# Attention and MLP block: the MLP's first input moved to SP's queue ahead of the last stores, W1 and v loads at other stages of the lead, Q loads for the maxima one slot earlier

## The chip, the core and the metric

The kernel runs on one core of a Trainium2 chip. The metric is device time in microseconds (us), the median of several runs. The engines are TensorE (PE, matmuls; PEld is its weight load), VectorE (DVE), ScalarE (ACT), GpSimd (POOL) and SyncE (SP). SP computes nothing; it issues most of the DMAs, in the order of its list, and stands still at an entry whose wait isn't met.

## The reference

```python
def _A_ref(x, wqkv, wo):                     # 1 x 2048 x 512, 32 heads of 16
    qkv = (x @ wqkv).reshape(B, S, 3, H, Dh).transpose(2, 0, 3, 1, 4)
    q, k, v = qkv[0], qkv[1], qkv[2]
    scores = einsum("bhqd,bhkd->bhqk", q, k) * (Dh ** -0.5)
    p = softmax(scores, axis=-1)
    o = einsum("bhqk,bhkd->bhqd", p, v)
    return o.transpose(0, 2, 1, 3).reshape(B, S, D) @ wo

def _B_ref(x, w1, b1, w2, b2):               # 512 -> 1792 -> 512
    h = einsum("bsd,df->bsf", x, w1) + b1
    r = where(h > 0, h, 0)
    return einsum("bsf,fd->bsd", r * r, w2) + b2

xn = layernorm(x)
out = x + _A_ref(xn, wqkv, wo) * silu(_B_ref(xn, w1, b1, w2, b2))
```

## The kernel before

Products are made from operands split in two parts, high and low, with three matmuls per product (`terms3`: high times high, high times low, low times high). Most matmuls use half of the PE's rows (64), so that two streams, called lanes, run side by side.

**Start.** Layer norm, transposes of the normed input into `xT`, and the first tiles of Q, K and V.

**Lead.** `lead_rounds` and `side_rounds` make the other Q, K and V tiles. Each tile is accumulated in PSUM, copied by ACT into `raw` (two buffers), split by POOL into `hl` (pool `hlp`, three buffers; lines L95 and L96), and stored by SP (`qk_store`, L943, into `q_d` or `k_d`) two rounds later. Between their matmuls PE makes maxima of the scores (`max_mm`, L316, reduced by DVE in L323) and, late in the lead, the first exponentials (`exp_mm`: scores L1192, then ACT L1204 into `pt`). The lead is counted in stages `g` of two maxima in each lane; 62 maxima per lane are made ahead. `mlp_early` opens buffers at stage 12; W1's first column blocks are loaded into `ex` (three buffers, `load_w1`, L453) and split by POOL into `w1s` (`split_w1`). `load_v` (L172) brings v for the first four heads. SPILLS writes `xT` out to `xn_d`. The last but one and the last tile of the lead have paths of their own: the last Q tile (`across`, in the bank `po`) is split quickly by ACT (L101) and DVE (L102) into a buffer of `hlp` and stored at once; the last K tile (`qk_done_last`) is copied by ACT into `ot` (L1012) and is split and stored some slots into the main loop.

**Main loop.** 512 slots `st`: 32 units (8 groups of four heads times four blocks of 512 queries) of 16 blocks of keys. A slot makes four maxima for later units, four exponentials, and the product of `pt` with v two slots back (L388, bank `po`). Between them lie the matmuls of the MLP (`mlp_tasks`), later those with wo. `first_pair` (L254) multiplies `xc`, a piece of 256 columns of the normed input from `xn_d`, with W1; `second` multiplies the result with W2. MLP blocks last four slots (`long_slots`). The first input `xc` is asked for at slot 2 by `load_xc(0)`, in four DMAs on ACT's queue (L503); the later ones on SP's.

**Q and K loads.** The maxima read Q from `qm` (a ring of three), the exponentials from `qe` (a ring of four). Both are loaded in pairs of heads, six DMAs each (L149), by `max_end(g)`: with `s` the stage within the unit, `qe` of unit u at s = 7 and 9, `qm` of unit u + 1 at s = 8 and 11 (unit 1 has stages of its own). A load into a ring waits until PE has read the buffer's old content.

The order of work on each engine is that of the program's text. On SP, DMAs use eight semaphores in turn, so an entry also waits for the one eight entries before it.

Of the kernel before, what the change touches and what calls it, by code (L numbers as in the profile page):

```python
# [10 lines left out]
F32R = mybir.dt.float32r  # L11
# [6 lines left out]
P = 128  # L18
# [17 lines left out]
EVAC_LAST = (1, 3, 4, 5, 7, 9)  # L36
GAPS = (18, 19, 20, 22)
FIRST = 2
SPILLS = (4, 7, 10, 13, 15, 17, 19, 21)
LAST_MAX = 486  # L40
PAIR = (484, 485)
# [12 lines left out]
def kernel(  # L54
# [11 lines left out]
    nc = tc.nc  # L66
# [44 lines left out]
    with ExitStack() as ph:  # L111
# [215 lines left out]
        def max_end(g):  # L327
            for u in [u for u, n in left.items() if n == 0]:
                del left[u]
                m4 = m4s[u % 2]  # L330
                nc.vector.tensor_reduce(m4[:, :16], mxs[u], axis=AX.X, op=ALU.max)
                mxs[u] = m4
                late.append((g + (6 if u else 0), u))
            u, s = divmod(g, 16)
            if u >= NU:
                return
            qd, qc = divmod(u, 4)
            if qc == 2 and qd + 1 < NQ and s % 2 == 0:
                load_k(qd + 1, s // 2)
            if qc == 3 and qd + 1 < NQ and s % 2 == 0 and s < 8:  # L340
                load_k(qd + 1, 8 + s // 2)
            at = (12, 14) if u == 1 else (7, 9)
            if s in at:
                load_q_pair(u, "qe", at.index(s), qes.setdefault(u, []))
            at = (6, 10) if u == 1 else (8, 11)
            if s in at and u + 1 < NU:
                load_q_pair(u + 1, "qm", at.index(s), qms.setdefault(u + 1, []))

# [119 lines left out]
        def mlp_tasks(mp):  # L468
# [29 lines left out]
            def load_xc(c):  # L498
                    xc = xp.tile([P, 2, KO, CW], F32R, name="xc")
                    for k in (0, 2) if c == 0 else (0,):  # L500
                        kos = slice(k, k + 2 if c == 0 else KO)
                        for i in range(2):
                            (nc.sync if c else nc.scalar).dma_start(  # L503
                                xc[:, i, kos].bitcast(F32), xn_d[i, :, kos, c * CW : (c + 1) * CW]
                            )
                    state["xc"] = xc
# [402 lines left out]
        pools = {}  # L909
# [89 lines left out]
        def qk_done(m, c, ps, quick, wait):  # L999
            hl = hlp.tile([P, 2, 512], F32R, name="hl")  # L1000
            if quick:
                split_psum(hl[:, 0], hl[:, 1], ps)
            else:
                raw = hlp.tile([P, 512], F32, name="raw", bufs=2)
                nc.scalar.activation(raw, ps, AF.Copy)
                split((hl[:, 0], hl[:, 1]), raw)
            later(wait, lambda: qk_store(m, c, hl))

        def qk_done_last(m, c, ps):

            raw = sp.tile([P, 512], F32, name="ot", bufs=1)
            nc.scalar.activation(raw, ps, AF.Copy)  # L1012

            def store():
                hl = pools["n"].tile([P, 2, 512], F32R, name="hl")
                split((hl[:, 0], hl[:, 1]), raw)
                later(3, lambda: qk_store(m, c, hl))

            last_store.append(store)

        def qk_first():
            tiles = [qk_tile(m, 0) for m in (4, 0)]
# [33 lines left out]
        def side_tile(spec, ps, end=None):  # L1056

            kind, a, b = spec
            if kind == "v":
                return v_terms(a, b, ps), lambda: v_done(a, b, ps, 1)  # L1060
            return qk_terms(a, b, ps), end or (lambda: qk_done(a, b, ps, False, 2))

        def side_rounds(specs, single):


            def half(tile_, lane, k):
                terms, _, first = tile_
                r = slice(64 * lane, 64 * lane + 64)
                out_, lh, rh, first_, last_ = terms[k]
                mm = nc.tensor.matmul(  # L1070
                    out_, lh(r), rh(r),
                    start=first_ and lane == first, stop=last_ and lane != first,
                    skip_group_check=True,
                )
                if k == 0 and lane != first:
                    tc.add_manual_dep(
                        mm.ins, since[first].ins.name,
                        mybir.DependencyInfo(
                            mybir.DependencyClass.Sync, mybir.DependencyReason.DATA
                        ),  # L1080
                        reason="the other row tile is done with the bank",
                    )

            n, behind, count = 3 * KO, 3 * KO // 2, len(specs) - 1
            (km, kc), tiles = specs[count][1:], {}
            ps = pv.tile([P, 512], F32, name="po")
            across = side_tile(specs[count], ps, lambda ps=ps: qk_done(km, kc, ps, True, 0)) + (1,)
            extra = [0, 0]
            for i in range(n * count + n + behind):
                if i % n == 0 and i // n < count:  # L1090
                    k = i // n
                    ps = pd.tile([P, 512], F32, name="pd_t") if k % 4 == 2 else pm.tile([P, 512], F32, name="pm_t")
                    end = None
                    if k == count - 1:
                        end = lambda ps=ps: qk_done_last(*specs[count - 1][1:], ps)
                    tiles[k] = side_tile(specs[k], ps, end) + (0,)
                for lane in range(2):
                    at = i - (n + behind) * lane
                    if 0 <= at < n * count:
                        half(tiles[at // n], lane, at % n)  # L1100
                        if lane and at % n == n - 1:
                            tiles.pop(at // n)[1]()
                        continue
                    e = extra[lane]
                    extra[lane] += 1
                    if lane:
                        if e % 3 == 2:
                            single(lane, "m")
                        else:
                            half(across, lane, e - e // 3)  # L1110
                    elif e < n:
                        half(across, lane, e)
                        if e == n - 1:
                            across[1]()
                    else:
                        single(lane, "sm"[e % 2], lambda: pm.tile([P, 512], F32, name="pm_t"))
                yield i + 1

        since = {}
        last_store = []  # L1120
# [224 lines left out]
        for g in range(LEAD):  # L1345
            shift_due(g)
            while min(made) < 2 * g + 2:
                next(rounds)
            max_end(g)
            if g == 0:  # L1350
                raw_r = [load_w("wv", 3 * P, ((D + P, 3 * P),))]
            if g == 3:
                for ko in range(KO):
                    split_w(wr_t, ko, slice(3 * P, 6 * P), raw_r[0][:, ko])
                ln.close()
                pools["v"] = ph.enter_context(tc.tile_pool(name="vp", bufs=1))
            if g == 12:
                s1.close()
                ep = ph.enter_context(tc.tile_pool(name="ep", bufs=1))
                rot["pt"] = [ep.tile([P, 512], F32, name=f"pt{i}") for i in range(NPT)]  # L1360
                pools["n"] = ph.enter_context(tc.tile_pool(name="np", bufs=1))
                mlp_early()
            if g in (18, 20):
                split_w1((g - 18) // 2)
                load_w1(3 + (g - 18) // 2)
            if g == 16:
                for fo in range(3):
                    load_w1(fo)
                load_v(0)
        for _ in rounds:  # L1370
            pass
# [161 lines left out]
        for st_ in range(NU * 16):  # L1533
            if st_ < done:
                continue
            begin(st_)
            if st_ == FIRST:
                qs.close()
            item = next(dn, None)
            if st_ == FIRST:  # L1540

                for g in (LEAD, LEAD + 1):
                    max_end(g)
                later(4, last_store.pop())
            if item is not None and len(item) > 2:
                assert st_ % 4 == 0
                long_slots(st_, *item[:2])
                done = st_ + 4
                continue
            if item is not None and item[0] is not None:  # L1550
                slot(st_, *item)
            else:

                plain_slot(st_)
                flip[0] += 1
            shift_due(st_ + 1 + LEAD)
            pv_step(st_ - 2, pts.pop(st_ - 2))
# [32 lines left out]
```

## Time and profile before

| | |
|---|---|
| median of 3 runs | 1638.53 us (1638.46 to 1638.76) |
| profiled execution, its own time | 1639.71 us |
| profiled execution, span | 1637.9 us |
| granted PE clock, mean over the span | 0.998 |
| HBM read, written | 149.95 MB, 56.61 MB |

In the profile's rows a start is counted from the span's first instruction. "SPq" and "ACTq" are DMA issues by SP and ACT, whose duration is that of the issue, not of the transfer. A row of a timeline gives start, duration, engine, line, operation, output and inputs, count, and in brackets the idle time before it with what ended it. A row of a stretch gives for each engine its busy time, with the count of its instructions, then the granted PE clock as a share of the full one, the busy share of the DMA engines, and GB/s. Two lanes run at once, so PE counts as busy when one of them stands.

### The profile page before, as it was taken

To read this page: it belongs to the slowest core of one execution; us is meant where nothing else is said; L and a number is where in the kernel's file an instruction comes from. 1 tells how busy PE (TensorE), PEld (TensorE's weight loads), DVE (VectorE), ACT (ScalarE), POOL (GpSimd) and SP (SyncE) were. 2 spreads that over 40 slices of the span, in tenths; PEclk is the share of its full clock that TensorE was granted. 3 is DMA by queue.
4 is the path that set the end of the run, shared out by engine and by line. 5 is a ranking of instruction groups with operands and counts; after the bars stand their busy time and mean duration, and the time that the engine had idled before them with its cause. 6 is when DMAs were issued, how large, how long until landed. Compare 5 with 4: busy or idle time off the path is not lost.

```text
span 1637.9 us, 36064 instructions
## 1 busy us (share of the span) xinstructions
PE 1617.7 (99%) x13684; PEld 941.6 (57%) x13684; DVE 1358.0 (83%) x2346; ACT 1189.5 (73%) x2351; POOL 523.3 (32%) x547
## 2 busy tenths in 40 slices
PE   8999999999999999999999999999999999999998
PEld 6898565456545654665566446644664565545543
DVE  6486788888888888888888988888888888887744
ACT  7212577777777777777777777777777777777786
POOL 6437568123212211231132113311331133225421
PEclk9999999999999999999999999999999999999999
DMA  6787555424333433433433334423442252246654
GB/s 229 222 277 256 176 184 154 117 85 143 81 86 98 125 75 97 122 96 82 105 108 98 87 93 118 120 63 89 136 114 52 85 156 76 56 129 198 200 171 155
DMA packets 163941, 209.22 MB, mean 128 GB/s; under 512 B 59448, under 2 KB 78392, under 8 KB 162232
## 3 DMA queue, kind: packets, MB, share of 16 engines
q1 hardware_dynamic: 162392, 205.35, 43.4%
q8 instruction: 108, 1.77, 0.5%
q10 hardware_dynamic: 1376, 1.57, 0.3%
q14 instruction: 65, 0.53, 0.1%
HBM read 149.95 MB, written 56.61 MB: 126 GB/s over the span
## 4 chain that ended last, share of the span: by engine, by line
PE 93%; ACT 3%; DMA 2%; SPq 1%; DVE 1%; POOL 1%; issue 0%; ACTq 0%; POOLq 0%; DVEq 0%
PE po L388 30%; PE pd_t L254 19%; PE pm_t L316 17%; PE se L1192 14%; PE pd_t L222 5%; PE pm_t L1070 3%; ACT pt L1204 2%; PE se L1040 1%; PE se L988 1%; DMA xc<-xn_d 1%; PE pd_t L1070 1%; DMA k_d<-hl 1%; PE se L316 1%; SPq L149 0%; PE pm_t L1154 0%; PE pd_t L1040 0%
## 5 line engine op out<-in xcount | busy, mean ns | idle before, releaser
L323 DVE TENSOR_REDUCE mx<-pm_t 128x1 f32<-128x512 f32 x1927 | 1196.9, 683 | 173.5 <-PE pm_t L316 83.9
L1204 ACT ACTIVATE pt<-se 128x512 f32<-128x512 f32 x1996 | 1043.2, 617 | 261.2 <-PE se L1192 214.0
L316 PE MATMUL pm_t<-ka,qm 64*128 64x512 f32 x1927 | 770.7, 420 | 2.5 <-DMA qm<-q_d 1.8
L1192 PE MATMUL se<-qe,ka 64*128 64x512 f32 x1996 | 672.9, 396 | 2.0 <-ACT pt L1204 2.0
L388 PE MATMUL po<-pt,v 128*32 128x512 f32 x4096 | 545.5, 605 | 0.0
L316 PEld LDWEIGHTS pm_t<-ka,qm 64*128 64x128 f32 x1927 | 338.6, 184 | 240.7 <-DVE mx L323 224.8
L254 PEld LDWEIGHTS pd_t<-xc,w1s 64*128 64x128 f32 x2688 | 335.4, 187 | 96.4 <-issue 89.0
L254 PE MATMUL pd_t<-xc,w1s 64*128 64x256 f32 x2688 | 382.1, 289 | 1.9 <-DMA xc<-xn_d 1.9
L1192 PEld LDWEIGHTS se<-qe,ka 64*128 64x128 f32 x1996 | 337.2, 185 | 22.0 <-ACT pt L1204 4.7
L254 PE MATMUL pd_t<-w2t,hT 64*128 64x512 f32 x1080 | 300.7, 411 | 0.0
L254 PEld LDWEIGHTS pd_t<-w2t,hT 64*128 64x128 f32 x1080 | 179.1, 184 | 83.0 <-issue 75.5
L546 POOL TENSOR_TENSOR r<-r 128x512 f32<-128x512 f32 x56 | 58.2, 1040 | 378.9 <-ACT r L543 378.9
L388 PEld LDWEIGHTS po<-pt,v 128*32 128x32 f32 x4096 | 81.0, 108 | 158.9 <-issue 136.5
L565 POOL TENSOR_TENSOR u<-u,b_t 128x512 f32<-128x512 f32 x16 | 20.6, 1286 | 318.4 <-ACT u L564 284.6
L426 POOL TENSOR_TENSOR ot<-ot,hl 128x512 f32<-128x512 f32 x31 | 39.9, 1287 | 201.9 <-DMA hl<-r_d 132.9
L323 DVE TENSOR_REDUCE mx<-se 128x1 f32<-128x512 f32 x121 | 77.9, 686 | 28.3 <-PE pm_t L1070 15.2
L222 PE MATMUL pd_t<-wot,oc 64*128 64x512 f32 x336 | 91.1, 407 | 0.0
L543 ACT ACTIVATE r<-pd_t,b_t 128x256 f32<-128x256 f32 x112 | 46.9, 470 | 57.1 <-PE pd_t L254 55.9
L222 PEld LDWEIGHTS pd_t<-wot,oc 64*128 64x128 f32 x336 | 58.2, 184 | 45.9 <-ACT pt L1204 12.6
L1070 PE MATMUL pm_t<-xT,wr_t 64*128 64x512 f32 x408 | 74.2, 388 | 0.0
L96 POOL TENSOR_TENSOR hT<-r,hT 128x512 fp32r<-128x512 f32 x56 | 72.3, 1291 | 4.7
L222 PE MATMUL pd_t<-w2t,hT 64*128 64x512 f32 x264 | 68.9, 393 | 0.0
(131 smaller groups left out, 1069.4 us busy)
## 6 DMA issues: line engine op xcount, KB each, us to landing
w1s<-w_d SPq DMA_DIRECT2D x196, 256.0 KB
qm<-q_d SPq DMA_DIRECT2D x384, 32.0 KB
ka<-k_d SPq DMA_DIRECT2D x96, 128.0 KB
qe<-q_d SPq DMA_DIRECT2D x384, 32.0 KB
k_d<-hl SPq DMA_DIRECT2D x16, 512.0 KB
q_d<-hl SPq DMA_DIRECT2D x16, 512.0 KB
xn_d<-xT SPq DMA_DIRECT2D x8, 1024.0 KB
g<-g_d SPq DMA_DIRECT2D x32, 256.0 KB
```

Source lines behind the costliest of these rows:

```text
L96: (lo or nc.gpsimd).tensor_tensor(dst[1], raw, dst[0].bitcast(F32), op=ALU.subtract)
L222: mm = nc.tensor.matmul(out_, lh(r), rh(r), start=first_ and lane == 0, stop=last_ and lane == 1, skip_group_check=True,)
L254: mm = nc.tensor.matmul(out_, lh(r), rh(r), start=first_ and lane == 0, stop=last_ and lane == 1, skip_group_check=True,)
L316: nc.tensor.matmul(ps, qms[u][p][64 * j : 64 * j + 64, qb * P : (qb + 1) * P], kas[qd, p][64 * j : 64 * j + 64, kc * 512 : (kc + 1) * 512] ...
L323: return nc.vector.tensor_reduce(mxs[u][:, c, kc : kc + 1], ps, axis=AX.X, op=ALU.max)
L388: nc.tensor.matmul(po[32 * j : 32 * j + 32, :], vs[qd][:, (4 * kb + j) * VW : (4 * kb + j) * VW + 32], pts[j], start=(kb == 0), stop=(kb = ...
L426: nc.gpsimd.tensor_tensor(ot, ot, hl[:, 1].bitcast(F32), op=ALU.mult)
L543: nc.scalar.activation(r[:, i], ps[:, i * CW : (i + 1) * CW], AF.Relu, bias=b1_t[:, fo : fo + 1])
L546: nc.gpsimd.tensor_tensor(r, r, r, op=ALU.mult)
L1070: mm = nc.tensor.matmul(out_, lh(r), rh(r), start=first_ and lane == first, stop=last_ and lane != first, skip_group_check=True,)
L1192: nc.tensor.matmul(se, kas[qd, j // 2][b : b + 64, kb * P : (kb + 1) * P], qes[u][j // 2][b : b + 64, :], start=True, stop=True,)
L1204: return nc.scalar.activation(pts[j], se, AF.Exp, scale=0.25)
```

## The change

- `load_xc(0)` issues its four DMAs on SP's queue, like the later ones. They stand there behind the lead's stores and ahead of the store of the last Q tile and of the Q loads that slot 2 asks for.
- The last Q tile (`qk_done_across`) is split into a buffer of the pool `n` in place of `hlp`, and its store is asked for at slot 2, behind `xc`. The last K tile's split and store use the same single buffer after it.
- W1's five first loads go out at stages 13, 14, 16, 20 and 23 in place of three at 16, one at 18 and one at 20; v at 18 in place of 16; the second W1 split at 21 in place of 20.
- `qm`'s first pair is asked for at s = 7 and `qe`'s first pair at s = 8, in place of 8 and 7.

The order of PE's and DVE's instructions is as before, and so is ACT's but for the four DMA issues. On SP the lead's stores and loads come in the text's order; before, some Q loads of the first slots stood among the lead's last stores, and now these stand behind `xc`.

```diff
+W1_LOADS = (13, 14, 16, 20, 23)
...
-            at = (12, 14) if u == 1 else (7, 9)
+            at = (12, 14) if u == 1 else (8, 9)
             if s in at:
                 load_q_pair(u, "qe", at.index(s), qes.setdefault(u, []))
-            at = (6, 10) if u == 1 else (8, 11)
+            at = (6, 10) if u == 1 else (7, 11)
             if s in at and u + 1 < NU:
                 load_q_pair(u + 1, "qm", at.index(s), qms.setdefault(u + 1, []))
...
                         for i in range(2):
-                            (nc.sync if c else nc.scalar).dma_start(
+                            nc.sync.dma_start(
                                 xc[:, i, kos].bitcast(F32), xn_d[i, :, kos, c * CW : (c + 1) * CW]
                             )
...
-            last_store.append(store)
+            last_store.append(lambda: later(4, store))
+
+        def qk_done_across(m, c, ps):
+            hl = pools["n"].tile([P, 2, 512], F32R, name="hl")
+            split_psum(hl[:, 0], hl[:, 1], ps)
+            last_store.append(lambda: qk_store(m, c, hl))
...
-            across = side_tile(specs[count], ps, lambda ps=ps: qk_done(km, kc, ps, True, 0)) + (1,)
+            across = side_tile(specs[count], ps, lambda ps=ps: qk_done_across(km, kc, ps)) + (1,)
...
-            if g in (18, 20):
-                split_w1((g - 18) // 2)
-                load_w1(3 + (g - 18) // 2)
-            if g == 16:
-                for fo in range(3):
-                    load_w1(fo)
+            if g in W1_LOADS:
+                load_w1(W1_LOADS.index(g))
+            if g in (18, 21):
+                split_w1((g - 18) // 3)
+            if g == 18:
                 load_v(0)
...
-                later(4, last_store.pop())
+                for fn in last_store:
+                    fn()
```

## The prediction

> **What bounds the kernel now.** I read the busy table first, then the waits of TensorE (PE), then the stretches of the span, then the timelines around each stretch in which PE is not full.
>
> ```profile
> span 1637.9 us, 36064 instructions
> PE 1617.7 (99%) x13684; PEld 941.6 (57%) x13684; DVE 1358.0 (83%) x2346; ACT 1189.5 (73%) x2351; POOL 523.3 (32%) x547
> ```
>
> PE is idle for 1637.9 - 1617.7 = 20.2 us in all. A change that leaves PE's instructions alone can win only there, and in time when PE runs below its pace. This one leaves them alone: PE, DVE and the activations keep their instructions and their order, only DMAs, some GpSimd (POOL) work and one evacuation's buffer move. So the question is which of these stretches it touches.
>
> ```profile
> core 0: us, PE busy (x) PEld busy (x) DVE busy (x) ACT busy (x) POOL busy (x), PEclk, DMA share, GB/s
> 138.00:150.00 12.00, 10.92 (x90) 8.94 (x88) 6.07 (x10) 3.78 (x8) 11.18 (x14) 1.00 0.88 307
> 170.00:181.00 11.00, 7.34 (x51) 3.36 (x49) 6.58 (x11) 5.71 (x11) 7.67 (x12) 0.98 0.97 297
> 177.00:180.40 3.40, 1.67 (x15) 0.96 (x11) 1.39 (x2) 1.28 (x3) 1.19 (x1) 1.00 1.13 340
> 180.40:183.80 3.40, 3.19 (x23) 2.97 (x27) 2.04 (x3) 1.42 (x3) 0.00 (x0) 0.53 0.48 125
> 184.00:319.00 135.00, 135.00 (x1190) 77.28 (x1186) 117.75 (x199) 102.70 (x205) 78.57 (x98) 1.00 0.49 146
> 318.90:322.30 3.40, 1.61 (x15) 0.72 (x15) 1.60 (x5) 1.44 (x3) 0.00 (x0) 1.00 0.35 101
> 322.00:1570.00 1248.00, 1248.00 (x10802) 689.02 (x10800) 1094.84 (x1864) 962.40 (x1907) 330.28 (x320) 1.00 0.39 107
> ```
>
> Between 184 and 1570 us PE is full but for one hole at 320. The three places to win are the end of the lead (138 to 150), the passage from the lead to the main loop (170 to 184, where the granted clock also falls to 0.53 for 3.4 us), and the hole at 320. The rest of the idle time lies at the first load and in the tail, which the change does not touch.
>
> **A: W1 and v loads spread over the lead.**
>
> ```profile
> 126.32 2.13 SPq L453 DMA_DIRECT2D ex<-in_B_w_dram  x3
> 128.50 0.59 SPq L172 DMA_DIRECT2D v<-v_d  x1
> ```
>
> ```profile
> 129.19 8.71 DMA k_d<-hl
> 167.13 2.78 DMA k_d<-hl
> ```
>
> ```profile
> 131.18 0.60 ACT L1005 ACTIVATE raw<-pd_t 128x512 f32<-128x512 f32 x1 [2.61 <-PE pd_t L1070]
> 140.07 0.60 ACT L1005 ACTIVATE raw<-pm_t 128x512 f32<-128x512 f32 x1 [4.25 <-POOL hl L96]
> ...
> 149.47 0.60 ACT L1005 ACTIVATE raw<-pm_t 128x512 f32<-128x512 f32 x1 [2.04 <-PE se L316]
> 152.69 0.60 ACT L1005 ACTIVATE raw<-pm_t 128x512 f32<-128x512 f32 x1 [2.13 <-PE se L316]
> ```
>
> The first fence is SP's queue, the second the chain of work (start, duration, what), the third ScalarE's timeline. Three W1 loads and the v load go out at once; the K store right behind them takes 8.71 us instead of 2.78. POOL's split waits for that store's buffer (three in the ring), the copies `raw` (two) wait for POOL, and the exponentials queued behind `raw` on ScalarE keep PE's banks. Both outer rows end a wait for PE, so they show PE's pace: a tile takes 152.69 - 149.47 = 3.22 us, and the five between 131.18 and 149.47 (135.22, 140.07, 144.41 and 146.34 lie in between) took 18.29, not 16.10. The loss is 2.2 us, of which 12 - 10.92 = 1.08 shows as idle; in the rest one of PE's two row halves ran alone. After the change W1 goes out at stages 13, 14, 16, 20 and 23 and v at 18, with at least one store between any two; the second W1 split on POOL comes one tile later. The v load's own delay stays, just before the exponentials begin: of the extra 8.71 - 2.78 = 5.9 us its 544 KB of 1312 KB (three loads of 256 KB and v) make 2.5 us, an estimate by bytes.
>
> ```profile
> 169.48 0.62 POOL L95 TENSOR_SCALAR hl<-raw 128x512 fp32r<-128x512 f32 x1 [0.41 <-ACT raw L1005]
> 170.18 1.30 POOL L96 TENSOR_TENSOR hl<-raw,hl 128x512 fp32r<-128x512 f32 x1
> ```
>
> POOL works 0.62 + 1.30 us in a tile of 3.22 and so makes up 1.3 us per tile, and the second copy gives another tile: most of 2.5 us is taken up before PE feels it. I take 0.3 us as left: gain **1.9**, bounds 2.2 and, if v hits the exponentials squarely (a rival below), 0; below zero would need more bytes at once than the 1312 KB of before, which the spreading excludes.
>
> **B: the passage, up to the MLP's first matmul.**
>
> ```profile
> 170.01 0.60 ACT L101 ACTIVATE hl<-po 128x512 fp32r<-128x512 f32 x1 [0.62 <-DMA k_d<-hl]
> ...
> 172.01 3.08 ACTq L503 DMA_DIRECT2D xc<-xn_d  x3
> 175.13 2.07 ACT L1204 ACTIVATE pt<-se 128x512 f32<-128x512 f32 x4 [2.57 <-PE pm_t L316]
> ```
>
> ```profile
> 172.04 0.49 PE L316 MATMUL pm_t<-ka,qm 64*128 64x512 f32 x1 [0.64 <-DVE mx L323]
> ...
> 175.78 0.50 PE L1192 MATMUL se<-qe,ka 64*128 64x512 f32 x1 [0.99 <-ACT pt L1204]
> ...
> 177.21 0.38 PE L254 MATMUL pd_t<-xc,w1s 64*128 64x256 f32 x1
> 178.37 0.38 PE L254 MATMUL pd_t<-xc,w1s 64*128 64x256 f32 x1 [0.67 <-DMA xc<-xn_d]
> ...
> 180.61 0.58 PE L254 MATMUL pd_t<-xc,w1s 64*128 64x256 f32 x1 [1.27 <-DMA xc<-xn_d]
> ...
> 183.68 1.20 PE L388 MATMUL po<-pt,v 128*32 128x512 f32 x8
> ...
> 186.94 0.50 PE L316 MATMUL pm_t<-ka,qm 64*128 64x512 f32 x1
> ...
> 189.53 1.06 PE L388 MATMUL po<-pt,v 128*32 128x512 f32 x8
> ```
>
> ScalarE issues the four transfers of `xc` itself: from 172.01 it stands at the last three for 3.08 us, and its exponentials go on at 175.13, which costs PE 0.99. On SP these issues are off ScalarE. The 0.64 is DVE being late: its half of the last tile's split follows ScalarE's at 170.01, which had waited for a K store's buffer. The tile now writes another buffer, so the wait goes; but only 0.62 us of ScalarE idleness lies there and part of it is PE finishing the tile, so I take 0.4. B: 0.99 + 0.4 = **1.4** of 1.63, bounds 0.9 and 1.63.
>
> **C: the wait for `xc`, and the clock.** From the first MLP matmul to the first `po` group: 183.68 - 177.21 = 6.47 us; the same part of the block at full pace takes 189.53 - 186.94 = 2.59. Loss 3.9 us: 0.67 + 1.27 of waits, about 3.19/2 = 1.6 of half clock, 0.4 of lone row halves. When does `xc` land from SP's queue?
>
> ```profile
> 171.87 0.86 SPq L943 DMA_DIRECT2D k_d<-hl  x1
> ```
>
> ```profile
> k_d<-hl SPq DMA_DIRECT2D x16, 512.0 KB
> ...
> xc<-xn_d ACTq DMA_DIRECT2D x4, 256.0 KB
> ```
>
> SP takes its list in order, and the last entry before `xc` is the K store (issued at 171.87 here) that waits for POOL's split, done at 170.18 + 1.30 = 171.5. That store lands after some 2.8 us, at 174.3; the four pieces behind it need 0.262 MB / 340 GB/s (the row from 177.00) = 0.77 us each, so they land at about 175.1, 175.8, 176.6 and 177.4. Before, the last landed by 180.6, because the same engines also moved another Q store of 512 KB, two W1 loads and six of Q: these now stand behind `xc` on SP. PE comes to the first matmul at 177.21 - 1.4 = 175.8, needs the second piece at once and the other two after six terms, which took from 178.37 to 180.61 - 1.27 = 179.34, about 1 us. So the fourth piece is late by 0.6 us; that much waiting remains. The half clock: it came behind a stretch with PE busy 1.67 of 3.40. The stretch 318.90 to 322.30 has 1.61 of 3.40 and no lower clock after it, so the trigger is not the share alone; with 0.6 us of waits instead of 1.9, and B's also gone, I take the fall as gone. C: 3.9 - 0.6 = **3.3**, bounds 0 and 3.9.
>
> What is queued behind SP's new wait (for PE's last matmul that reads the memory `xc` takes): the Q store of the last tiles, `qm` and `qe` loads of the next units and two W1 loads. The nearest need is `qm`: 62 maxima per row half are made ahead, two more in each slot from 2 on, and its pair begins with number 80, nine slots on, at 5.8 us for two slots (189.53 - 183.68) some 26 us later. The last K tile now shares one buffer with the tile before and its split waits for that store; POOL has no other work there until the first MLP activation, and nothing near reads that K.
>
> **D: Q for the maxima one slot sooner.**
>
> ```profile
> 297.42 1.73 SPq L435 DMA_DIRECT2D on_d<-hl  x4
> 307.12 2.63 SPq L149 DMA_DIRECT2D qe<-q_d  x6
> 309.79 1.46 SPq L172 DMA_DIRECT2D v<-v_d  x1
> ...
> 314.14 3.96 SPq L149 DMA_DIRECT2D qm<-q_d  x6
> ```
>
> ```profile
> 321.75 0.46 PE L316 MATMUL pm_t<-ka,qm 64*128 64x512 f32 x1 [1.79 <-DMA qm<-q_d]
> ```
>
> SP was free from 299.2 but stood until 307.12 at the `qe` load, whose buffer PE was still reading. `qm` came behind that, behind v and two `xc` pieces. Swapped, `qm` finds its buffer long free (its last maxima lie some 12 slots back) and goes out near 299.2; even if it takes the 7.6 us that it took here (314.14 to 321.75) it is there at 307, 13 us before PE asks (321.75 - 1.79 = 319.96). `qe` goes one slot later, and its unit starts 16 slots after. The swap is made in nearly all 32 units; elsewhere PE shows no such hole, so it neither gains nor costs there. D: **1.8**, bounds 1.5 and 1.8.
>
> **Sum.** 1.9 + 1.4 + 3.3 + 1.8 = 8.4 us. After 184 us PE is the full engine (135.00 of 135.00), so each us won ahead arrives at the end. The profiled execution took 1639.71 us, its span 1637.9: span after 1629.5, that execution 1631.3. The median shown is 1638.53, 1.2 below the profiled one: **1630.1**.
>
> **The rivals.**
> 1. `xc` still comes late and the clock falls as before: C brings nothing, 1638.5 - (1.9 + 1.4 + 1.8) = 1633.4. It decides if SP reaches `xc` 3 us later than I take it, for example one POOL tile of 3.22 us behind. Against: POOL ended the last split 0.1 us after PE's last tile. [...] Chance 0.14.
> 2. The clock falls although the waits go: 1.6 less, 1631.7. What speaks for it: the longest single wait before the fall was only 1.27 us, and a hole of 1.79 at 320 made no fall, so the waits need not be its cause. [...] Chance 0.08.
> 3. The lead's stall moves: v now lands among the first exponentials, A brings nothing: 1632.0. Chance 0.09.
> 4. Slower: SP's one list. If POOL falls two tiles (6.4 us) behind in the lead, SP stands at its stores, and two more of them than in my sum (1.05 MB, 3.1 us) go out at once ahead of `xc`, whose last piece lands at 177.4 + 6.4 + 3.1 = 186.9, against a need at 177: 9.9 us of waiting and a window at half clock (1.7) in place of C's 3.9. With B won, D won and A's loss kept: 1638.5 + 11.6 - 3.9 - 1.4 - 1.8 = 1643.0. The balance tips at a wait of 7.1 - 1.7 = 5.4 us (7.1 is C, B and D together), a lag of some 3.4 us with its share of stores, and it is slower by over 0.2% from about 5.6 us; POOL would have to lose that where the spreading should save. Chance 0.05.
> 5. The gain is swallowed (a new wait in the 31 reordered units, 0.27 us in each): 1638.5. Against: every other unit has PE full in either order. Chance 0.06.
>
> **How the numbers follow.** Forecast 0.58, rivals 0.14, 0.08, 0.09, 0.05, 0.06. A measurement of this kernel can tell about 0.2% (3.3 us) from no change, so faster means under 1635.2: forecast and rivals 1 to 3 nearly whole, 0.88 with a little taken off for a mix of 1 and 3; same 0.07; slower 0.05. All losses gone would be 2.2 + 1.63 + 3.9 + 1.8 = 9.5, or 1629.0; the low end is 1628.8. The high end takes in rivals 1 and 3 together, 1635.3.
>
> **What would show it.** Right: PE's holes at 141 and 145, 172 to 181 and 320 gone or under 0.7 us, no stretch with clock under 1.00 between 60 and 1620, no K store over 6 us, `qm` issued before v near 300. Wrong: `xc` landing after 179, ScalarE's `raw` waiting for POOL beyond 150, a new PE wait for `qe` or `qm`.

## The result and the profile after

| | before | changed |
|---|---|---|
| median (runs) | 1638.49 us (8) | 1633.93 us (8) |
| lowest to highest | 1637.21 to 1641.77 | 1633.35 to 1635.61 |
| profiled execution, its own time | 1639.71 us | 1634.46 us |
| profiled execution, span | 1637.9 us | 1632.7 us |

The ratio is 0.9971, interval 0.9961 to 0.9982. The change made the kernel faster by 4.6 us. The forecast was 1630.1 us, a gain of 8.4; the direction and the range held, the size was about twice too large.

The busy table of the changed kernel has the same work on every engine. PE's idle time is 1632.7 - 1616.6 = 16.1 us, where it was 20.2.

```profile
span 1632.7 us, 36089 instructions
PE 1616.6 (99%) x13684; PEld 943.5 (58%) x13684; DVE 1358.6 (83%) x2346; ACT 1189.7 (73%) x2351; POOL 523.3 (32%) x547
```

The waits of PE (total us, times, longest):

```profile
PE pd_t L255 <- DMA xc<-xn_d: 1.5, 3, 0.7
...
PE pd_t L223 <- DMA oc<-on_d: 0.4, 1, 0.4
PE pm_t L317 <- DVE mx L324: 0.4, 1, 0.4
PE se L1198 <- ACT pt L1210: 0.3, 1, 0.3
```

The wait for `qm` (1.8) is gone, that for ScalarE's exponentials has fallen from 2.0 to 0.3, and a wait for `oc` is new. The wait for `xc` should have fallen to 0.6 and stands at 1.5. The same stretches as in the prediction, for the changed kernel:

```profile
core 0: us, PE busy (x) PEld busy (x) DVE busy (x) ACT busy (x) POOL busy (x), PEclk, DMA share, GB/s
138.00:150.00 12.00, 12.00 (x108) 11.93 (x106) 7.37 (x12) 4.07 (x8) 10.24 (x13) 1.00 0.78 245
170.00:181.00 11.00, 9.40 (x62) 4.44 (x60) 6.97 (x12) 5.47 (x10) 5.81 (x9) 0.84 0.69 221
177.00:180.40 3.40, 3.40 (x27) 2.25 (x25) 1.99 (x3) 1.79 (x3) 1.89 (x2) 0.57 0.29 82
180.40:183.80 3.40, 3.40 (x30) 1.58 (x28) 2.00 (x4) 1.58 (x3) 0.00 (x0) 0.93 0.58 154
184.00:319.00 135.00, 135.00 (x1190) 77.42 (x1186) 119.50 (x203) 104.47 (x208) 78.56 (x98) 1.00 0.57 162
318.90:322.30 3.40, 3.40 (x30) 1.41 (x24) 2.71 (x6) 2.03 (x4) 0.00 (x0) 1.00 0.02 5
322.00:1570.00 1248.00, 1247.27 (x10792) 687.61 (x10790) 1092.17 (x1859) 962.51 (x1909) 332.76 (x321) 1.00 0.39 106
```

PE is full at 138 to 150 and at 320, where the holes were. The half clock is still there: at 177.00 to 180.40 the granted clock is 0.57 and in the next stretch 0.93, so (0.43 + 0.07) x 3.4 = 1.7 us of PE time are lost.

To place the gain I cut the way to the steady loop at four events of PE's timeline: the first matmul of the side tiles, the end of the lead's last matmul, the first MLP matmul (T0), and the second `po` group after T0. "Half clock" says whether the stretch behind T0 has a window of some 3.4 us with the granted clock near 0.5. The runs with names are told in the next section.

| profile | start | lead | end of lead to T0 | T0 to second `po` group | half clock |
|---|---|---|---|---|---|
| before | 62.78 | 108.62 | 5.81 | 8.73 | yes |
| e10, before again | 64.65 | 106.94 | 6.02 | 8.55 | yes |
| changed | 62.89 | 106.42 | 4.28 | 8.57 | yes |
| e7, changed again | 63.20 | 106.32 | 4.24 | 6.87 | no |
| e11, changed, third | 63.60 | 106.32 | 4.42 | 6.77 | no |
| e1, Q swap alone | 64.23 | 106.88 | 5.87 | 7.33 | no |
| e2, loads spread alone | 63.81 | 106.30 | 5.76 | 8.51 | yes |
| e3, passage alone | 64.29 | 107.88 | 4.15 | 8.73 | yes |
| e6, `xc` on SP alone | 64.39 | 106.71 | 5.50 | 8.59 | yes |
| e4, K store behind `xc` | 63.19 | 106.40 | 4.12 | 6.49 | no |
| e12, both stores behind | 63.27 | 106.40 | 4.13 | 5.76 | no |
| e8, order of terms | 64.60 | 106.31 | 4.12 | 5.82 | no |
| e9, swap to unit 27 | 64.19 | 106.32 | 4.11 | 4.70 | no |
| e5, a quarter of `xc` | 64.40 | 106.31 | 4.35 | 4.71 | no |

The first pair of profiles differs by 5.2 us: 2.2 in the lead (A), 1.5 up to T0 (B), 0.2 behind T0 (C), 1.8 at 320 (D), less 0.1 for a later start and 0.45 for the wait for `oc` near 1513. Step C, forecast at 3.3, brought nothing in this execution.

### The profile page after: what moved, and what is told of

Its sections match the earlier page's. It is cut to its first block, busy times and chain, and to the rows that moved or that the text cites. A ratio compares the mean times of both kernels' runs of the same rounds, so it can differ in the third digit from the quotient of the medians.

```text
span 1632.7 us, 36089 instructions
## 1 busy us (share of the span) xinstructions
PE 1616.6 (99%) x13684; PEld 943.5 (58%) x13684; DVE 1358.6 (83%) x2346; ACT 1189.7 (73%) x2351; POOL 523.3 (32%) x547
## 4 chain that ended last, share of the span: by engine, by line
PE 98%; DVE 1%; DMA 1%; SPq 0%; issue 0%; ACT 0%; POOL 0%; DVEq 0%; POOLq 0%; ACTq 0%
PE po L389 31%; PE pd_t L255 19%; PE pm_t L317 17%; PE se L1198 14%; PE pd_t L223 6%; PE pm_t L1076 4%; PE pd_t L1076 1%; PE se L1046 1%; PE se L989 1%; PE se L317 1%; PE pm_t L1198 1%; PE pm_t L1160 0%; DVE mx L324 0%; PE pd_t L1046 0%; PE pm_t L829 0%; DMA xc<-xn_d 0%
```

## The experiments

Ratios are to the kernel before, timed on the same chip.

| kernel | median us (runs) | ratio, interval | span of its profile |
|---|---|---|---|
| e1, Q swap alone | 1637.02 (10) | 0.9991, 0.9982 to 1.0000 | 1635.7 |
| e2, loads spread alone | 1638.04 (10) | 0.9996, 0.9987 to 1.0005 | 1636.1 |
| e3, passage alone | 1635.45 (10) | 0.9982, 0.9973 to 0.9991 | 1635.7 |
| e6, `xc` on SP alone | 1638.05 (11) | 0.9999, 0.9990 to 1.0008 | 1636.3 |
| e7, changed again | 1633.01 (7) | 0.9972, 0.9961 to 0.9983 | 1630.6 |
| e4, K store behind `xc` | 1631.79 (5) | 0.9964, 0.9951 to 0.9976 | 1629.9 |
| e12, both stores behind | 1631.58 (5) | 0.9963, 0.9948 to 0.9977 | 1629.3 |
| e8, order of terms | 1632.24 (5) | 0.9963, 0.9950 to 0.9975 | 1631.6 |
| e9, swap to unit 27 | 1632.36 (8) | 0.9969, 0.9959 to 0.9980 | 1629.8 |
| e5, a quarter of `xc` | 1630.18 (5) | 0.9952, 0.9939 to 0.9966 | 1629.1 |

**e1 to e3: the three parts, one at a time.** Each is the kernel before with one part of the change.

```diff
 e1:
-            at = (12, 14) if u == 1 else (7, 9)      # qe
+            at = (12, 14) if u == 1 else (8, 9)
...
-            at = (6, 10) if u == 1 else (8, 11)      # qm
+            at = (6, 10) if u == 1 else (7, 11)
 e2:
+W1_LOADS = (13, 14, 16, 20, 23)
...
-            if g in (18, 20):
-                split_w1((g - 18) // 2)
-                load_w1(3 + (g - 18) // 2)
-            if g == 16:
-                for fo in range(3):
-                    load_w1(fo)
+            if g in W1_LOADS:
+                load_w1(W1_LOADS.index(g))
+            if g in (18, 21):
+                split_w1((g - 18) // 3)
+            if g == 18:
                 load_v(0)
 e3:
-                            (nc.sync if c else nc.scalar).dma_start(
+                            nc.sync.dma_start(
...
+        def qk_done_across(m, c, ps):
+            hl = pools["n"].tile([P, 2, 512], F32R, name="hl")
...
```

> The kernel before with the Q swap alone (qm's first pair at s = 7, qe's at s = 8). Theory: the hole of 1.79 us at 320 goes and nothing else moves, span 1637.9 - 1.8 = 1636.1, the passage at 170 to 184 and its half clock as before. Rival (the swap only moves the wait, to qe or to another load): a new PE wait of over 1 us somewhere after 300, span near 1637.9.

> The kernel before with W1 and v loads spread alone. Theory: the lead's last matmul ends near 169.3 in place of 171.4, PE without idle between 126 and 165, then the passage and the hole at 320 as before, span 1637.9 - 2.1 = 1635.8. Rival (the passage takes it back: xc meets the same stores and comes no sooner): lead's end 2.1 us sooner, but the first po group of the MLP's first block still at 183.7, span near 1637.9.

> The kernel before with xc on SP and the last Q tile's other buffer and later store, without the other parts. Theory (xc stands behind a K store of 512 KB on SP and still lands late, the clock falls): first MLP matmul 1.5 us sooner after the lead's end than before (4.3 us in place of 5.8), some 1.5 us of waits for xc, a half-clock window, span 1637.9 - 1.7 = 1636.2. Rival (the passage's gain in the changed kernel came only because the lead ran smoothly): no gain, 1637.9.

The swap brings 1638.63 - 1637.02 = 1.6 us (interval 0 to 2.9), the loads 0.6 with an interval that takes in none, the passage 3.2 (1.5 to 4.4). Together 5.4, about what the whole change gives (0.9971 and 0.9972 are 4.6 to 4.8); within this noise there is no sign that the parts fight each other. In the profiles each part does its own work: with the swap the hole at 320 is gone, with the spread the lead is 106.30, and with the passage the second stage is 4.15.

**e6: `xc` on SP, and nothing else.** The last Q tile keeps its buffer and is stored at once, so its store stands ahead of `xc`.

```diff
-                            (nc.sync if c else nc.scalar).dma_start(
+                            nc.sync.dma_start(
```

> The kernel before with xc on SP alone, the last Q tile stored at once as before and so ahead of xc with the K store. Theory (what counts is the bytes ahead of xc on SP): ScalarE is free, so the first MLP matmul comes 4.5 us after the lead's end in place of 5.8; xc stands behind 1 MB and waits come to about 3 us (1.6 us more than in the changed kernel), so nearly all of the 1.3 us is given back; span 1637.9 within 1. Rival (freeing ScalarE is all that the move brings, the order behind the stores does not matter): waits as in the changed kernel, 1.5 us, span near 1636.2.

It brings nothing that can be measured. SP's queue, and PE's timeline behind it:

```profile
167.97 3.35 SPq L943 DMA_DIRECT2D q_d<-hl  x2
171.42 0.42 SPq L943 DMA_DIRECT2D k_d<-hl  x1
171.93 3.31 SPq L503 DMA_DIRECT2D xc<-xn_d  x4
```

```profile
176.60 0.35 PE L254 MATMUL pd_t<-xc,w1s 64*128 64x256 f32 x1 [0.82 <-POOL hl L95]
177.17 0.39 PE L254 MATMUL pd_t<-xc,w1s 64*128 64x256 f32 x1 [0.22 <-DMA xc<-xn_d]
```

ScalarE is freed here too, but `xc` now stands in SP's list behind a K store that waits for POOL's last split, and the last Q tile's 512 KB go out ahead of it too. The row puts the 0.82 down to POOL, whose split just before it, from 175.94 to 176.56, is that of the last K tile; these matmuls read only `xc` and `w1s`, so I take it for the wait for the first piece of `xc`. What ScalarE no longer loses is lost at T0 instead: the stage to T0 takes 5.50, only 0.3 to 0.5 below the profiles of before. The other buffer and the later store of the last Q tile, taken together, are what make the move pay (4.15 in e3); no run has one without the other.

**e4, e5 and e12: what stands beside `xc`.** The changed kernel with edits at the passage only. e4 holds the K store that goes out just ahead of `xc` (its tile in a buffer of v that is not yet used) and stores it behind `xc`. e12 also asks for that store and for the last Q store two slots later. e5 loads only the first of the four parts of the first `xc` and uses it for all four; it shows the passage without a wait for `xc`.

```diff
 e4:
+        def qk_done_held(m, c, ps):
+            raw = hlp.tile([P, 512], F32, name="raw", bufs=2)
+            nc.scalar.activation(raw, ps, AF.Copy)
+            hl = vs["tiles"][1][:, :1024].bitcast(F32R).rearrange("p (a n) -> p a n", a=2)
+            split((hl[:, 0], hl[:, 1]), raw)
+            last_store.append(lambda: qk_store(m, c, hl))
...
+                    if k == count - 2:
+                        end = lambda ps=ps: qk_done_held(*specs[count - 2][1:], ps)
 e12, on e4, in qk_done_held and in qk_done_across:
-            last_store.append(lambda: qk_store(m, c, hl))
+            last_store.append(lambda: later(2, lambda: qk_store(m, c, hl)))
 e5:
-                    for k in (0, 2) if c == 0 else (0,):
-                        kos = slice(k, k + 2 if c == 0 else KO)
+                    for k in (0,):
+                        kos = slice(k, k + 1 if c == 0 else KO)
...
-                            lambda b, q, ko=ko: xc[q, b, ko],
+                            lambda b, q, ko=ko: xc[q, b, ko if c else 0],
```

> The changed kernel, with the last K store that stands ahead of xc on SP moved behind it: that tile is split into the second v tile, free until slot 48, and stored after xc. Theory (the 512 KB ahead cost xc 1.6 us, and the waits bring the half clock): waits for xc under 0.4 us in place of 1.5, no half-clock window before 1620, span 1632.7 - 1.2 - 1.7 = 1629.8. Rival 1 (the waits aren't the cause of the half clock): waits gone but the window at 0.5 stays, span 1631.4. Rival 2 (xc is late by its own start and pace, not by the store): waits stay at 1.5 us, span 1632.7.

> The changed kernel, but the first input of the MLP is loaded for a quarter only (two pieces of 128 KB), and the first piece's matmuls all read that quarter: it leaves out three quarters of the first load, so the wait for xc is taken away by less data. Theory (the half clock comes from PE's waits around xc): PE waits for xc under 0.3 us in all, from the first MLP matmul to the second po group some 4.9 us, no half-clock window before 1620, span 1632.7 - 3.6 = 1629.1. Rival (the clock falls for the thin work of slots 2 and 3, whatever xc does): the window at 0.5 stays in most executions, mean clock 0.999 or less, span near 1630.8.

> As e4_store_behind, but the held K store and the last Q tile's store are asked for two slots later, so that they stand behind the six qm loads (0.2 MB) in SP's list: nothing but these small loads is then in flight while xc (four pieces, 1.05 MB) moves. In e4 the pieces were still 0.78 + 0.30 = 1.1 us late. Between 170.5 and 176.4 us its DMA engines moved 5.90 us x 315 GB/s = 1.86 MB, 0.8 MB more than xc has, so the stores behind xc in SP's list were served before xc's last piece. Theory (the stores behind take their share of the engines): without them xc and qm are 1.25 MB, 3.7 us at 340 GB/s from the start of transfers, so the last piece lands some 2 us sooner than in e4 and PE's waits for xc are under 0.3 us; the stage from the first MLP matmul to the second po group after it takes 4.7 to 5.4 us instead of 6.5. Rival (xc's own pace: it is slow whatever stands behind it, by its short rows or its issues): the waits stay at 0.8 to 1.1 us, the stage at 6.2 to 6.6, and GB/s in that stretch falls to about 200. By the median 1630.0 to 1631.5 by the theory, 1631.5 to 1632.5 by the rival, with the spread between executions making the stage the better sign.

First the changed kernel itself: SP's queue, PE's timeline, and the stretches of the passage with the bytes that the DMA engines moved (last column).

```profile
169.41 0.36 SPq L944 DMA_DIRECT2D k_d<-hl  x1
169.88 2.47 SPq L504 DMA_DIRECT2D xc<-xn_d  x4
172.45 0.41 SPq L944 DMA_DIRECT2D q_d<-hl  x1
172.91 3.68 SPq L150 DMA_DIRECT2D qm<-q_d  x6
```

```profile
169.74 0.50 PE L317 MATMUL pm_t<-ka,qm 64*128 64x512 f32 x1 [0.44 <-DVE mx L324]
...
173.59 0.35 PE L255 MATMUL pd_t<-xc,w1s 64*128 64x256 f32 x1
174.51 0.38 PE L255 MATMUL pd_t<-xc,w1s 64*128 64x256 f32 x1 [0.57 <-DMA xc<-xn_d]
...
176.19 0.35 PE L255 MATMUL pd_t<-xc,w1s 64*128 64x256 f32 x1 [0.72 <-DMA xc<-xn_d]
176.76 0.38 PE L255 MATMUL pd_t<-xc,w1s 64*128 64x256 f32 x1 [0.21 <-DMA xc<-xn_d]
...
182.16 1.06 PE L389 MATMUL po<-pt,v 128*32 128x512 f32 x8
```

```profile
169.50:170.00 0.50, 0.26 (x2) 0.19 (x2) 0.50 (x2) 0.50 (x2) 0.42 (x2) 1.00 0.00 0
170.00:171.50 1.50, 1.40 (x12) 0.34 (x10) 1.50 (x4) 1.50 (x3) 1.42 (x3) 1.00 0.83 298
171.50:174.50 3.00, 2.44 (x18) 0.77 (x14) 2.63 (x5) 1.10 (x3) 2.50 (x5) 1.00 0.92 262
174.50:176.80 2.30, 1.35 (x11) 0.87 (x11) 0.84 (x2) 1.08 (x2) 0.00 (x0) 1.00 0.99 355
```

The list is in the order that was meant. But by 176.8 us, when the last piece of `xc` is there, the engines have moved 1.50 x 298 + 3.00 x 262 + 2.30 x 355 = 2050 KB, where the K store and `xc` are 524 + 1049 = 1573 KB. The other 0.48 MB, 1.4 us at 340 GB/s (the kernel before, 177.00 to 180.40), can only be what was issued behind `xc`: the Q store at 172.45 and the `qm` loads. So the engines were working on later entries before PE had the last piece. But 0.48 MB is only the most that can have been served ahead of `xc`. Had everything gone in the order of the list, the 1573 KB would have been through by about 175.5 (1.50 x 298 + 3.00 x 262 + 1.0 x 355), and the other 1.3 us would then be time between the last byte and PE's start. The trace does not say which bytes were whose, so the two accounts are not told apart here.

e4 and e12, PE's timeline in each:

```profile
175.68 0.35 PE L255 MATMUL pd_t<-xc,w1s 64*128 64x256 f32 x1 [0.78 <-DMA xc<-xn_d]
176.34 0.38 PE L255 MATMUL pd_t<-xc,w1s 64*128 64x256 f32 x1 [0.30 <-DMA xc<-xn_d]
```

```profile
175.71 0.38 PE L255 MATMUL pd_t<-xc,w1s 64*128 64x256 f32 x1 [0.48 <-DMA xc<-xn_d]
```

In e4 the waits are 1.1 us, against 1.2 to 1.5 in the three profiles of the changed kernel, and the stage behind T0 is 6.49, against 6.8 to 6.9 in the two without half clock. In e12 they are 0.48 and 5.76. Without any wait for `xc` the stage is 4.71 (e5), so late data costs 2.1 us in the changed kernel (6.77 and 6.87 less 4.71). The medians bear that out: e5 lies 2.8 us below e7, taken on the same chip (1630.18 against 1633.01), and every execution of e5 is faster than every one of e7. How those 2.1 us divide between the store ahead, the stores beside and `xc` itself is not shown. Each step is a difference of two single profiles, and e8 and e9 below, which have the same passage, differ by more (5.82 and 4.70). PE's timeline in e8, then in e9:

```profile
177.71 0.38 PE L255 MATMUL pd_t<-xc,w1s 64*128 64x256 f32 x1 [0.35 <-DMA xc<-xn_d]
```

```profile
176.15 0.40 PE L255 MATMUL pd_t<-xc,w1s 64*128 64x256 f32 x2
```

These rows are the fourteenth term of e8 and the thirteenth and fourteenth of e9, the first to read the last two pieces. SP issues `xc` from 170.94 on in e8 and from 170.53 on in e9. So from the first issue of `xc` to its last piece pass 6.77 us in e8, as in e4 (6.72), but under 5.9 in e9, whose list on SP is the same, with both stores right behind `xc`. That is no longer than in e12 without them (6.00). And e4 and e12 have the same ratio by the median (0.9964 and 0.9963). So e12 does not decide between the two theories that I gave it. The stretches of e12 show how the load runs when nothing but the `qm` loads stands beside it:

```profile
170.00:171.00 1.00, 0.79 (x4) 0.37 (x4) 1.00 (x3) 1.00 (x3) 0.92 (x3) 1.00 0.20 48
171.00:172.00 1.00, 1.00 (x10) 0.16 (x8) 1.00 (x3) 0.87 (x2) 0.92 (x2) 1.00 1.00 331
...
174.00:175.00 1.00, 1.00 (x11) 0.72 (x9) 0.88 (x3) 0.44 (x1) 0.57 (x1) 1.00 0.57 188
175.00:176.00 1.00, 0.52 (x4) 0.32 (x6) 0.61 (x2) 0.64 (x2) 0.00 (x0) 1.00 0.44 158
```

`xc` was asked for from 169.71 on; little moves before 171, the engines are full for 3 us, and then they stand half empty while PE waits until 175.71. The forecast had 1.26 us for start and end together, inside the 2.8 us that it gave the K store (2.8 less 524 KB at 340 GB/s); what makes the slow start and end was not tried.

**e8: the order of the terms.** On e4, the first MLP pair multiplies what has already landed before what is still missing.

```diff
+                if c == f == 0:
+                    mms = mms[:6] + mms[12:18] + mms[6:12] + mms[18:]
```

> The changed kernel with the last K store behind xc, and in the first MLP pair both column halves use the first two pieces of xc before either uses the last two: twelve terms in place of six are done before the third piece is needed, one more us of work. Theory: the waits that the store behind xc left (0.78 and 0.30 us) go, from the first MLP matmul to the second po group about 5.2 us in place of 6.49, span 1629.9 - 1.1 = 1628.8. Rival (the waits were partly hidden by the other row half, so the order changes nothing): span 1629.9.

The stage behind T0 falls from 6.49 to 5.82, but, as said, it is 4.70 in e9 with the same passage, so one profile does not give the size of the step. By the median nothing is gained over e4 (ratios 0.9963 and 0.9964). The profile of e8 shows a loss at another place. PE's timeline, SP's queue, and the chain of waits:

```profile
1512.39 0.49 PE L223 MATMUL pd_t<-wot,oc 64*128 64x512 f32 x1 [0.82 <-DMA oc<-on_d]
```

```profile
1503.96 4.02 SPq L150 DMA_DIRECT2D qe<-q_d  x6
1508.02 0.42 SPq L676 DMA_DIRECT2D oc<-on_d  x1
```

```profile
1505.23 0.42 SPq L150
1505.69 1.82 SPq L150
1507.55 0.42 SPq L150
```

The later `qe` load of the swap stands ahead of an `oc` load in SP's list, and one of its six issues takes 1.82 us instead of 0.42. The wait for `oc` is 0.45 in the first profile of the changed kernel, 0.60 in e1, and absent in e4, e5, e7, e11 and e12. None of the profiles without the swap has it, so it goes with the swap, in some executions. Slow issues alone do not make it: in e4 the same six take 3.88 us together, against 4.02 in e8 and 2.61 in e11, and PE has no wait.

**e9: the swap only up to unit 27,** on e8, to free that place.

```diff
-            at = (12, 14) if u == 1 else (8, 9)
+            at = (12, 14) if u == 1 else (8, 9) if u < 28 else (7, 9)
...
-            at = (6, 10) if u == 1 else (7, 11)
+            at = (6, 10) if u == 1 else (7, 11) if u < 28 else (8, 11)
```

> The kernel with the store behind xc and the new order of terms, and the Q swap only up to unit 27; the last units load qe first again, as before. Theory (the late wait for oc, 0.4 to 0.8 us near 1510 in three profiles with the swap, comes from the two qe loads now standing together ahead of that oc piece): no wait for oc over 0.2 us, the oc piece asked for some 1.5 us sooner against PE, span 0.5 to 0.8 less than with the swap throughout. Rival (that wait depends on other traffic): it stays.

The wait for `oc` is gone, and one for `qm` stands late in the loop instead. From the waits of PE in e9:

```profile
PE pm_t L317 <- DMA qm<-q_d: 0.3, 1, 0.3
```

No gain follows. Of the versions that leave nothing out, e4 and e12 have the lowest medians, but their intervals and that of the changed kernel overlap.

**e7, e10 and e11: the same kernels again,** to see what differs between executions of one program.

> The changed kernel once more, for a second profile. [...] Rival (the fall is fixed in the program's order): the same window behind xc as in the first profile.

> The kernel before once more, for a second profile. Theory (the lead's loss and the fall of the clock differ from execution to execution): the lead takes between 106.5 and 108.6 us from its first side matmul to its last, waits for xc again near 2 us, the hole at 320 again 1.0 to 1.8 us; the half clock as it falls. Rival (both are fixed): 108.6 and a half-clock window again.

> The changed kernel a third time, for its profile. Theory: the lead takes 106.3 to 106.5 us again, waits for xc 1.3 to 1.5 us, and the half clock as it falls, with a span near 1632.7 where it does and near 1631 where it doesn't. Rival: the lead's time or the waits for xc vary as much as in the kernel before.

e7 waits for `xc` nearly as long as the first profile of the changed kernel (1.3 against 1.5), in the same places. Its stretch behind the waits:

```profile
176.00:179.40 3.40, 2.98 (x28) 1.95 (x28) 1.89 (x3) 1.57 (x3) 1.14 (x2) 1.00 0.59 211
```

The clock is 1.00. So the fall is not fixed by the program. In e11 the clock is 1.00 as well, with 1.2 us of waits. The stage behind T0 is 6.87 without the fall and 8.57 with it: 1.7 us, the same as worked out from the granted clock. Among the profiles with 1.2 us or more of waits for `xc`, six have the window (before, e10, e2, e3, e6, changed; granted clock 0.91 from 165 to 184) and three have not (e1 with 2.0 us of waits, e7, e11; 1.00 there); of the five with 1.1 us or less (e4, e5, e8, e9, e12; 1.00 there) none has.

e10 shows that the kernel before differs too: its lead takes 106.94, not 108.62. Its span is 1638.3 us, that of e11 1630.8; both were run once.

## Why the prediction was right or wrong

**Direction, and the rule that a us won ahead arrives at the end: right.** PE is full from 184 to 319 and nearly so to 1570, and the stage gains of the first pair of profiles add up to the difference of the spans within 0.1 us.

**A, 1.9: the mechanism right, the size the top of what occurs.** ScalarE's timeline of the changed kernel:

```profile
131.29 0.60 ACT L1006 ACTIVATE raw<-pd_t 128x512 f32<-128x512 f32 x1 [2.56 <-POOL w1s L97]
...
147.38 0.60 ACT L1006 ACTIVATE raw<-pm_t 128x512 f32<-128x512 f32 x1 [2.15 <-PE pm_t L1076]
150.59 0.60 ACT L1006 ACTIVATE raw<-pm_t 128x512 f32<-128x512 f32 x1 [2.12 <-PE pm_t L1076]
```

Five tiles take 147.38 - 131.29 = 16.09 us, the pace of 3.22 each, and from 147 on the copies wait for PE. All of the 2.2 came; the 0.3 that I kept back for v did not show. But the nine profiles with the spread have a lead of 106.30 to 106.42, and the five with the old loads 106.71 to 108.62, mean 107.4: the stall that I measured was the largest of the five. On average A is worth 1.1, and e2's median agrees (0.6, with an interval from -0.8 to 2.1 us). The step that failed is "the loss is 2.2 us", read from one execution and taken for all.

**B, 1.4: the sum right, one term too large.** It measured 1.5 to 1.6. ScalarE's stop of 0.99 at T0 is gone. DVE's 0.64, counted with 0.4 for the new buffer, is only down to 0.44, and e6, which keeps the old buffer, has 0.49; the other 0.3 of B lies elsewhere in the passage and was not placed. e6 adds that without the last Q tile's new buffer and later store hardly any of B is left.

**C, 3.3: mis-sized.** In the first profile it brought 0.2. Two steps failed. The first is "so they land at about 175.1, 175.8, 176.6 and 177.4", that is, the last 5.9 us after POOL's split, which lets the K store go. The K store went out as early before T0 as forecast (173.59 - 169.41 = 4.2, forecast 175.8 - 171.5 = 4.3), so rival 1's condition, SP reaching `xc` 3 us late, did not hold. The last piece came 176.76 - 169.41 = 7.4 us after that store, and 7.2 in e7 and e11: 1.3 to 1.5 later than forecast. I gave `xc` the full 340 GB/s in the order of the list; the engines moved less (262 GB/s from 171.5 to 174.5), and up to 0.48 MB of what they moved was not ahead in the list. How much of the delay is this share, and how much is time between the last byte and PE's start, stays open. The waits were 1.2 to 1.5 in place of 0.6.

The second is "I take the fall as gone". It came in one of three profiles of the changed kernel, and in e3, which has the same passage. Rival 2 had it come although the waits go; the waits had not gone, so it was not put to the test. Where they did fall below 1.2 us (e4, e5, e8, e9, e12), no profile has the fall. The four profiles with the old passage (before, e10, e1, e2) take 8.3 us on average behind T0, the four with the new one (changed, e7, e11, e3) 7.7, so C is 0.5 by these; the fall came in three of the first four and two of the second. By the medians, e3 brings 3.2 (1.5 to 4.4) for B and C, of which B is 1.5 to 1.6, so C is about 1.6, with an uncertainty as wide.

**D, 1.8: right in the first pair.** Over the five profiles without the swap the hole at 320 is 1.0 to 1.8 us (1.8, 1.6, 1.5, 1.0, 1.2), mean 1.4; with the swap it is gone in all. The prediction saw no cost in the other units. One came, the wait for `oc` of 0 to 0.8 us near 1512, where the list of SP has other loads to pass. e1's median gain, 1.6 (0 to 2.9), is the net.

**The rivals.** Rival 1's sum, 1633.4, is nearest to the median, and its outcome (`xc` late, the clock falls) is that of the first profile; its cause was another, as said. Rival 3 (the stall moves to the exponentials), rival 4 (POOL far behind) and rival 5 (a wait in each unit) have nothing in the traces: the lead is shorter (106.42 against 108.62), POOL's splits are not late (the last one ahead of `xc` lets its store go out at 169.41, 0.1 us after the lead's last matmul), and PE is full in the loop (1247.27 of 1248.00).

**The sum.** With A 1.1, B 1.6, C 0.5 to 1.6, D 1.4 and 0.2 off for `oc` (three waits over eight profiles with the full swap), the gain is 4.4 to 5.5 us; the medians gave 4.6 and, as part gains, 5.4. The forecast was 3.8 us too high: 0.8 of it lies in A, 0.6 in D with the wait for `oc`, and the rest, the largest part, in C. That the time fell inside the range owes something to luck: its upper half comes from rivals 1 and 3, and the causes that these name did not occur.

## What to carry to other kernels

A landing time worked out from the bytes ahead in one queue's list and a full rate can be too early: here it gave 5.9 us and 7.2 to 7.4 were measured, while the engines were already moving what stood behind. A stall read from a single execution can be the largest of its kind (here a lead of 108.62 us, where five profiles have 106.71 to 108.62); before a term of 2 us is counted in full, see it in two or three executions. The same holds for an experiment: two profiles of the same passage differed by 1.1 us here, more than the steps that e4 and e12 were to show. When a load is moved off a busy engine, look at what then stands ahead of it on the new queue: here the move alone gave nothing that could be measured (e6, ratio 0.9999), and the other buffer and later store of one tile made it pay (e3, 0.9982).

## What the runs showed of the hardware

- The half clock came after waits of at most 1.3 us each, in some executions and not in others of the same kernel, and cost 1.4 to 1.7 us (8.73 against 7.33 and 8.57 against 6.87). In the first profiles of both kernels the granted clock was 0.50 for 3.4 us (180.57 to 183.98 before, 177.44 to 180.85 changed) and 1.00 just ahead of it and just behind. A hole of 1.79 us at 320 in the kernel before made no fall: the clock is 1.00 in every us from 314 to 330. Why the fall comes in some executions only was not shown.
- One issue of a 32 KB load on SP took 1.82 us among others of 0.42 (e8), and one 1.81 in the first profile of the changed kernel. The six issues there take 4.02 and 4.00 us together, 4.09 in e1, 3.88 in e4 and 2.61 in e11. What held it stays open.
- The first matmul of the side tiles starts between 62.8 and 64.7 us in these profiles, whatever the edit. This spread of 1.9 us is one reason why versions that differ by less than 1 us (e4, e8, e9, e12) can't be ranked by five to eight executions each.
